# Fourteen early expert visits, one read of the last channels' matrix, and the tiles that go with them

## The chip, the cores and the metric

The kernel runs on one core of one Trainium2 chip. The metric is device microseconds (us) of one execution. In the tables, PE is TensorE's matmul stream and PEld its weight loads, DVE is VectorE, ACT is ScalarE, POOL is GpSimd and SP is SyncE; a name with a small q (SPq, POOLq) is the engine's queue, which issues DMAs and waits on semaphores. PEclk is the clock that TensorE was granted, as a share of 2.4 GHz; its two levels are 1.2 and 2.4 GHz.

## What is computed

```python
# x: 8 x 2880 x 192, fp32.  A causal 7-tap filter with softmaxed weights, one filter per head of 24 channels
out = np.einsum('hk,bskhg->bshg', w, x_unf)
x = out.reshape(23040, 192)
# 16 experts in 4 groups of 4: top-1 group, then top-1 expert in it
g_idx = np.argmax(x @ w_group, axis=1)
...
e_idx = np.argmax(xg @ w_expert[g], axis=1)
...
h = np.maximum(xg[mask_e] @ w1[g, e], 0.0)          # 192 -> 1024
ye = h @ w2[g, e]                                    # 1024 -> 192
out[tok_idx] = (g_w * e_w)[:, None] * ye
```

So each of the 23040 tokens is filtered, sent to one of 16 experts, and its expert's output is scaled by two softmax factors. The experts get between 1252 and 1628 tokens with these inputs.

## The kernel before, in words

**Routing.** The tokens are cut into 18 units of at most 12 blocks of 120 tokens. A unit (function `unit`) loads its x, filters it on TensorE with a banded matrix (L486), copies the result out with ACT (L495), transposes it, forms the logits, finds the expert on DVE, counts the position of every token in its expert's list, writes the filtered rows to a DRAM table `xcd` and scatters the token numbers into a DRAM table `idtab` by an indirect DMA of POOL (L699, with the row numbers in the small tile `rowi`, written by POOL on L678, and the token numbers in `lsi`, written by DVE on L696). A unit is a generator with 24 to 47 stages; `step()` runs one stage of one live unit.

**Visits.** The experts' work is done in visits. A visit reads one expert's matrices (`weights`): the first 128 of the 192 input channels of w1 into `ra` (512 KB), the last 64 channels into `rb`, and the two halves of w2 into `rc` (384 KB each). `rb` is filled twice from the same rows of w1, once in partitions 0 to 63 (L731) and once in 64 to 127 (L732), 256 KB each. All of these are issued on the SP queue, in order, into three `raw` buffers and three `rawc` buffers. `split` then cuts each matrix into a high part (ACT, L753, L757, L764) and the rest (DVE, L754, L758, L765), because the matmuls run in fp32r. One matmul with the high part `bh` and one with the rest `bl` take the right-hand side `xb`, whose one half of the partitions holds the high part of the last 64 channels of the tokens and whose other half holds the rest of them.

**Order.** An early visit takes tokens of an expert before all are routed. There are three portions of early visits (`VISITS`): ten experts with one slot of 256 tokens, from unit 5 on; three with two slots, from unit 9 on; three with three slots, from unit 12 on. That is 25 slots, and each is one pass of the main loop with `hidden` and `back`. While a slot runs, `advance(rate[0])` is called 16 times and runs stages of the units that are still to be routed; the rate is worked out anew at each slot:

```python
rate[0] = max(
    [(stages_to(portions[q][0]) - done[0]) / (max(starts[q] - MARGIN - i, 1) * 2 * NF)
     for q in starts if q not in idps] + [0.0])
```

with `MARGIN` 3, `NF` 8, `i` the slot that is being opened (two ahead of the one that runs) and `starts[q]` the slot at which portion q starts. A portion is opened by a read of its lists from `idtab` on the SP queue (L1197).

When all units are routed, `close_table` ends the lists: DVE writes the tile `rowi` (L948), which has the same two buffers as the units' `rowi`, and POOL scatters the end marks. Then come the wide portion (expert 0, four tiles of 128) and the last portion, in which the experts are visited in the order of what they have left (`RANKS`: the groups of tiles of each rank; `ROWS_OF`: the rows of a tile). There a group of two to four tiles goes through `hidden_pair` and `back_pair` together, eight steps a group. A branch at the end would run further visits if a rank had more tokens than its tiles hold.

Of the kernel before, what the change touches and what calls it, by code (L numbers as in the profile page):

```python
# [20 lines left out]
P = 128  # L21
BT = 120
# [15 lines left out]
def conv_moe_kernel(  # L38
# [60 lines left out]
    VISITS = ((NEED, 1, 10), (9, 2, 3), (12, 3, 3))  # L99
    portions, given = [], []  # L100
    for need, spe, n in VISITS:
        portions.append((need, tuple((len(given) + k, (2,) * spe) for k in range(n))))
        given += [2 * spe] * n
    assert len(given) == E
# [4 lines left out]
        (4, 4, 3), (4, 4, 3), (4, 4, 3), (4, 3, 3), (4, 3, 3), (4, 3, 3), (3, 3, 3), (3, 3, 3),  # L109
        (4, 4), (4, 4), (4, 3), (4, 3), (3, 3), (3, 3), (3, 2), (3, 2),  # L110
    )
    assert len(RANKS) == E
    ROWS_OF = (126, 126, 120, 120, 120, 120, 128, 124, 128, 126, 118, 114, 126, 118, 128, 116)
# [268 lines left out]
    first = [wsp.tile([P, 4, F], F32R, name="wf")]  # L382
    x_room()
    wm = const.tile([P, H], F32, name="wm")
# [48 lines left out]
    def unit(u, pre=None):  # L433
# [241 lines left out]
        rowi = rt.tile([P, 1], I32, name="rowi")  # L675
# [6 lines left out]
        def list_products():  # L682
            pl = bank("l")
            nrep = REPO if u < REPU else 1
            for k in range(nb):
                nc.tensor.matmul(
                    out=pl[:, 0:nrep * LH].rearrange("p (r n) -> p r n", r=nrep),
                    lhsT=ohl[0:Q, k // BI, :, :, k % BI].rearrange("p e l -> p (e l)"),
                    rhs=ohr[0:Q, k // BI, :, k % BI].unsqueeze(1).broadcast_to([Q, nrep, LH]),
                    start=k == 0, stop=k == nb - 1,  # L690
                )
            lv5 = rt.tile([P, LH], F32, name="lv5", bufs=1)
            lsi = rt.tile([P, LH], I32, name="lsi")
            nc.vector.tensor_scalar(
                out=lv5, in0=pl[:, 0:LH], scalar1=0.0, scalar2=float(BIG), op0=ALU.is_equal, op1=ALU.mult)
            nc.vector.scalar_tensor_tensor(  # L696
                out=lsi, in0=pl[:, 0:LH], scalar=float(t0 - 1), in1=lv5, op0=ALU.add, op1=ALU.add)

            nc.gpsimd.indirect_dma_start(  # L699
                out=TABV, out_offset=bass.IndirectOffsetOnAxis(ap=rowi.bitcast(U32), axis=0),  # L700
                in_=lsi, in_offset=None,
            )
            finished(u)
# [9 lines left out]
    def weights(r1, r2, spare=False, part=False):  # L713
# [16 lines left out]
        def load_b():  # L730
            hold(first_one, nc.sync.dma_start(out=rb[0:D2], in_=w1f[bass.ds(r1 + P, D2), :]))  # L731
            hold(first_one, nc.sync.dma_start(out=rb[D2:P], in_=w1f[bass.ds(r1 + P, D2), :]))  # L732
# [15 lines left out]
        def split(k):  # L748
            if k == 0:
                W["all"] = first.pop() if first else wsp.tile([P, 4, F], F32R, name="wf")  # L750
                W["ah"], W["al"], W["bh"], W["bl"] = (W["all"][:, q] for q in range(4))
# [3 lines left out]
            elif k == 1:  # L755
                bh, bl = W["bh"], W["bl"]
                hold(fix, pin(not fix, nc.scalar.activation(out=bh, in_=rb, func=AF.Copy)))  # L757
                hold(fix, nc.vector.tensor_tensor(out=bl, in0=rb, in1=bh.bitcast(F32), op=ALU.subtract))  # L758
# [49 lines left out]
    def turn(xs, n=2, packed=False, into=None, single=False, m=P):  # L808
# [18 lines left out]
        if packed:  # L827
            for t in range(2):
                hi, lo = slice(t * D2, (t + 1) * D2), slice((1 - t) * D2, (2 - t) * D2)
                cs = slice(t * m, (t + 1) * m)  # L830
                pb = px[hi, SLOT:SLOT + m]
                nc.scalar.activation(out=xb[hi, cs], in_=pb, func=AF.Copy)
                nc.vector.tensor_tensor(out=xb[lo, cs], in0=pb, in1=xb[hi, cs].bitcast(F32), op=ALU.subtract)  # L833
# [109 lines left out]
    def close_table():  # L943
        rows = rt.tile([P, E + 1], F32, name="rows")
        rowi = rt.tile([P, 1], I32, name="rowi")
# [482 lines left out]
    with tc.If(nrare[0] != 0):  # L1428
# [5 lines left out]
        with tc.For_i(0, nover, 1):  # L1434
            for u in range(NU):
# [5 lines left out]
                idw = rt.tile([P, LH], I32, name="lsi")[0:BT, 0:nb]  # L1441
# [72 lines left out]
```

## Time and profile before

| | |
|---|---|
| median of 3 runs | 1094.79 us (1093.23 to 1101.34) |
| the profiled execution | 1095.49 us, of which the span in the trace is 1093.7 us |
| PE busy | 1043.5 us (95%) |
| DVE, ACT, POOL busy | 676.4, 583.0, 521.4 us |
| mean granted TensorE clock | 0.986 |
| moved by DMA | 135.06 MB, 123 GB/s over the span |

Engines run beside each other, so the shares don't add up to one. TensorE's busy time is what is nearest to the span; the rows further down show in which stretches the rest of the span lies. All rows are of the one profiled execution, with times from the start of its span.

### The profile page before, as it was taken

The numbers are of one execution on the slowest core, as the hardware profiler recorded it, in microseconds if no ns is written. First come the engines' busy times: TensorE is split into PE (matmuls) and PEld (weight loads), VectorE is DVE, ScalarE is ACT, GpSimd is POOL, SyncE is SP. The second block draws the span as 40 slices with busy tenths as digits, with TensorE's granted clock in tenths as the row PEclk, the third lists the DMA queues.
The fourth block names the chain that finished last, engine by engine and source line by source line (L and its number), as shares of the span: only waits on it lengthen the run. The fifth ranks groups of instructions, "written<-read, shape, count | busy, mean of one in ns | idle before, by whom it ended". The sixth has DMA issues, their size and how long they took to land.

```text
span 1093.7 us, 20735 instructions
## 1 busy us (share of the span) xinstructions
PE 1043.5 (95%) x7116; PEld 981.0 (90%) x7116; DVE 676.4 (62%) x1646; ACT 583.0 (53%) x1346; POOL 521.4 (48%) x676
## 2 busy tenths in 40 slices
PE   6878999989999989999999999999999999999996
PEld 6756898889999889799999999999999999999996
DVE  4666887876777765666564645556466466655652
ACT  6565676676666634545454545545455455545552
POOL 3132333433333445755555554555546656657642
PEclk9998999999999989999999999999999999999998
DMA  8968799997675433432322313143233344334300
GB/s 233 252 151 222 206 244 246 234 212 181 174 181 137 105 92 110 132 100 60 93 70 79 105 40 103 45 109 94 59 105 68 85 103 111 71 85 102 92 24 24
DMA packets 122922, 135.06 MB, mean 123 GB/s; under 512 B 21147, under 2 KB 107424, under 8 KB 122810
## 3 DMA queue, kind: packets, MB, share of 16 engines
q1 hardware_dynamic: 75322, 79.89, 28.7%
q0 software_dynamic: 24160, 35.99, 12.3%
q10 hardware_dynamic: 23328, 17.80, 6.9%
q8 instruction: 57, 0.93, 0.4%
q14 instruction: 55, 0.45, 0.1%
HBM read 97.68 MB, written 36.07 MB: 122 GB/s over the span
## 4 chain that ended last, share of the span: by engine, by line
PE 79%; DMA 11%; DVE 4%; issue 2%; ACT 2%; POOL 0%; SPq 0%; POOLq 0%; ACTq 0%; DVEq 0%
PE ph L857 27%; PE po L871 10%; PE ph L887 8%; PE pm L871 8%; PE po L875 5%; PE po L905 5%; PE pm L875 3%; PE pm L486 3%; DMA xcd<-xc 3%; DMA raw<-in_moe_w 2%; PE po L909 2%; DMA out<-ys,idp 2%; DMA rawc<-in_moe_w 1%; PE ph L820 1%; DMA xg<-xcd,idp 1%
## 5 line engine op out<-in xcount | busy, mean ns | idle before, releaser
L924 POOL DMA_INDIRECT out<-ys,idp x187 | 213.1, 1140 | 271.6 <-DVE ys L934 218.6
L861 DVE SCALAR_TENSOR_TENSOR hl<-ph,hh 128x360 fp32r<-128x360 f32 (+13 forms) x328 | 189.3, 583 | 200.1 <-ACT hh L860 199.7
L860 ACT ACTIVATE hh<-ph 128x360 fp32r<-128x360 f32 (+13 forms) x328 | 167.3, 514 | 220.9 <-PE ph L857 214.4
L784 POOL DMA_INDIRECT xg<-xcd,idp x187 | 222.3, 1189 | 72.9 <-issue 28.4
L871 PE MATMUL po<-cw,hh 128*120 128x384 f32 (+6 forms) x656 | 209.7, 357 | 0.0
L857 PE MATMUL ph<-xa,wf 128*128 128x360 f32 (+13 forms) x656 | 182.6, 359 | 0.0
L857 PE MATMUL ph<-xc,wf 128*128 128x360 f32 (+13 forms) x656 | 176.1, 349 | 1.3 <-DVE xc L833 1.3
L875 PE MATMUL po<-cw,hl 128*120 128x192 f32 (+6 forms) x656 | 164.6, 251 | 0.0
L871 PE MATMUL pm<-cw,hh 128*120 128x384 f32 (+6 forms) x440 | 147.3, 356 | 0.0
L905 PE MATMUL po<-cw,hh 128*128 128x384 f32 x400 | 135.6, 389 | 0.0
L857 PEld LDWEIGHTS ph<-xc,wf 128*128 128x128 f32 x656 | 118.8, 188 | 10.6 <-DVE xc L833 1.5
L875 PEld LDWEIGHTS po<-cw,hl 128*120 128x120 f32 (+6 forms) x656 | 121.7, 186 | 3.0
L871 PEld LDWEIGHTS po<-cw,hh 128*120 128x120 f32 (+6 forms) x656 | 120.4, 184 | 2.8
L887 PE MATMUL ph<-xa,wf 128*128 128x256 f32 x600 | 118.5, 306 | 1.0 <-DVE wf L754 1.0
L857 PE MATMUL ph<-lts,wf 128*128 128x360 f32 (+13 forms) x328 | 114.9, 350 | 0.0
L875 PE MATMUL pm<-cw,hl 128*120 128x192 f32 (+6 forms) x440 | 110.3, 251 | 0.0
L909 PE MATMUL po<-cw,hl 128*128 128x192 f32 x400 | 102.0, 255 | 0.0
L857 PEld LDWEIGHTS ph<-xa,wf 128*128 128x128 f32 x656 | 100.7, 189 | 1.2
L887 PEld LDWEIGHTS ph<-xa,wf 128*128 128x128 f32 x600 | 88.5, 192 | 7.7 <-issue 2.3
L893 DVE SCALAR_TENSOR_TENSOR hl<-ph,hh 128x512 fp32r<-128x512 f32 x100 | 68.2, 685 | 41.2 <-ACT hh L892 40.9
L887 PE MATMUL ph<-xb,wf 128*128 128x256 f32 x400 | 81.9, 286 | 7.3 <-DVE xb L833 5.1
L892 ACT ACTIVATE hh<-ph 128x512 fp32r<-128x512 f32 x100 | 59.4, 598 | 53.6 <-PE ph L887 53.1
(274 smaller groups left out, 1864.2 us busy)
## 6 DMA issues: line engine op xcount, KB each, us to landing
rawc<-in_moe_w SPq DMA_DIRECT2D x66, 384.0 KB
raw<-in_moe_w SPq DMA_DIRECT2D x33, 512.0 KB
raw<-in_moe_w SPq DMA_DIRECT2D x66, 256.0 KB
xcd<-xc ACTq DMA_DIRECT2D x13, 1085.6 KB
xin<-in_x SPq DMA_DIRECT2D x7, 1134.0 KB
xin<-in_x SPq DMA_DIRECT2D x5, 1039.5 KB
xg<-xcd,idp POOLq DMA_INDIRECT x187
out<-ys,idp POOLq DMA_INDIRECT x187
```

Source lines behind the costliest of these rows:

```text
L784: nc.gpsimd.indirect_dma_start(out=xs[t][0:m, 0:XW], out_offset=None, in_=xcd[0:known, :], in_offset=bass.IndirectOffsetOnAxis(ap=ids[0:m, ...
L857: nc.tensor.matmul(out=hp, lhsT=W[wgt][:, fs], rhs=xx[:, 0:n], start=i == 0, stop=i == len(ops) - 1)
L860: nc.scalar.activation(out=hh, in_=hp, func=AF.Relu)
L861: nc.vector.scalar_tensor_tensor(out=hl, in0=hp, scalar=0.0, in1=hh.bitcast(F32), op0=ALU.max, op1=ALU.subtract,)
L871: nc.tensor.matmul(out=oo[t][0:m, 0:2 * D], lhsT=hh[:, ts], rhs=cw[:, f].rearrange("p a d -> p (a d)"), start=f == 0, stop=False,)
L875: nc.tensor.matmul(out=oo[t][0:m, 0:D], lhsT=hl[:, ts], rhs=cw[:, f, 0, :], start=False, stop=f == NF - 1,)
L887: nc.tensor.matmul(out=hp[:, j], lhsT=wgt[:, fs], rhs=xx, start=i == 0, stop=i == len(ops) - 1)
L892: nc.scalar.activation(out=hh, in_=hp, func=AF.Relu)
L893: nc.vector.scalar_tensor_tensor(out=hl, in0=hp, scalar=0.0, in1=hh.bitcast(F32), op0=ALU.max, op1=ALU.subtract,)
L905: nc.tensor.matmul(out=oo[t][:, 0:2 * D], lhsT=hh[:, j, ts], rhs=cw[:, f].rearrange("p a d -> p (a d)"), start=f == 0, stop=False,)
L909: nc.tensor.matmul(out=oo[t][:, 0:D], lhsT=hl[:, j, ts], rhs=cw[:, f, 0, :], start=False, stop=f == NF - 1,)
L924: nc.gpsimd.indirect_dma_start(out=outviews[nscat[0] % len(outviews) if view is None else view], out_offset=bass.IndirectOffsetOnAxis(ap=i ...
```

## The change

The early portions become seven experts with one slot, three with two and four with three: again 25 slots, in fourteen visits, and the last two experts get none. `RANKS` and `ROWS_OF` change with what is left for each rank; the last visit has two groups of two tiles where it had one of three and one of two. Both versions have 133 tiles in the last portion, in 40 groups, and the same sum of rows, 16300.

The last 64 channels of w1 are read once. ACT writes their high part twice, into either half of the partitions of `bh`, from the one copy; DVE forms the rest for the lower half of `bl` alone, and the upper half is zero, written once for each of the two `wf` buffers by POOL (`next_wf`). `turn` with `packed` puts both tiles' high parts into the lower half of `xb`, as the unpacked form does already. The two products that change are the rest of a weight times the rest of a token, which falls away for all tokens.

The tiles `rowi` and `lsi` of the units get four buffers instead of two, and `close_table` a tile of its own, `rowl`. The buffer of `wf` that holds the x of units 5 and 6 at first is taken ahead of the first weights' buffer instead of behind it.

```diff
-    VISITS = ((NEED, 1, 10), (9, 2, 3), (12, 3, 3))
+    VISITS = ((NEED, 1, 7), (9, 2, 3), (12, 3, 4))
...
+    given += [0] * (E - len(given))
...
-        (4, 4, 3), (4, 4, 3), (4, 4, 3), (4, 3, 3), (4, 3, 3), (4, 3, 3), (3, 3, 3), (3, 3, 3),
-        (4, 4), (4, 4), (4, 3), (4, 3), (3, 3), (3, 3), (3, 2), (3, 2),
+        (4, 4, 4), (4, 4, 3), (4, 4, 3), (4, 4, 3), (4, 4, 3), (4, 3, 3), (4, 3, 3), (3, 3, 3),
+        (4, 4), (4, 3), (4, 3), (3, 3), (3, 3), (3, 2), (3, 2), (2, 2),
...
-    ROWS_OF = (126, 126, 120, 120, 120, 120, 128, 124, 128, 126, 118, 114, 126, 118, 128, 116)
+    ROWS_OF = (124, 126, 126, 124, 120, 120, 120, 128, 118, 122, 114, 128, 124, 128, 112, 124)
...
-    first = [wsp.tile([P, 4, F], F32R, name="wf")]
     x_room()
+    wfs = [wsp.tile([P, 4, F], F32R, name="wf")]
+    nsplit = [0]
+
+    def next_wf():
+        k = nsplit[0]
+        nsplit[0] += 1
+        if k == 1:
+            wfs.append(wsp.tile([P, 4, F], F32R, name="wf"))
+        if k < 2:
+            nc.gpsimd.tensor_scalar(
+                out=wfs[k][D2:P, 3].rearrange("p (f q) -> p f q", q=P),
+                in0=ident[D2:P].unsqueeze(1).broadcast_to([D2, NF, P]), scalar1=0.0, scalar2=None, op0=ALU.mult)
+        return wfs[k % 2]
...
-        rowi = rt.tile([P, 1], I32, name="rowi")
+        rowi = rt.tile([P, 1], I32, name="rowi", bufs=4)
...
-            lsi = rt.tile([P, LH], I32, name="lsi")
+            lsi = rt.tile([P, LH], I32, name="lsi", bufs=4)
...
             hold(first_one, nc.sync.dma_start(out=rb[0:D2], in_=w1f[bass.ds(r1 + P, D2), :]))
-            hold(first_one, nc.sync.dma_start(out=rb[D2:P], in_=w1f[bass.ds(r1 + P, D2), :]))
...
-                W["all"] = first.pop() if first else wsp.tile([P, 4, F], F32R, name="wf")
-                W["ah"], W["al"], W["bh"], W["bl"] = (W["all"][:, q] for q in range(4))
+                w = next_wf()
+                W["ah"], W["al"], W["bh"], W["bl"] = (w[:, q] for q in range(4))
...
-                hold(fix, pin(not fix, nc.scalar.activation(out=bh, in_=rb, func=AF.Copy)))
-                hold(fix, nc.vector.tensor_tensor(out=bl, in0=rb, in1=bh.bitcast(F32), op=ALU.subtract))
+                for half in (slice(0, D2), slice(D2, P)):
+                    hold(fix, pin(not fix, nc.scalar.activation(out=bh[half], in_=rb[0:D2], func=AF.Copy)))
+                hold(fix, nc.vector.tensor_tensor(
+                    out=bl[0:D2], in0=rb[0:D2], in1=bh[0:D2].bitcast(F32), op=ALU.subtract))
...
-                hi, lo = slice(t * D2, (t + 1) * D2), slice((1 - t) * D2, (2 - t) * D2)
                 cs = slice(t * m, (t + 1) * m)
-                pb = px[hi, SLOT:SLOT + m]
-                nc.scalar.activation(out=xb[hi, cs], in_=pb, func=AF.Copy)
-                nc.vector.tensor_tensor(out=xb[lo, cs], in0=pb, in1=xb[hi, cs].bitcast(F32), op=ALU.subtract)
+                pb = px[t * D2:(t + 1) * D2, SLOT:SLOT + m]
+                nc.scalar.activation(out=xb[0:D2, cs], in_=pb, func=AF.Copy)
+                nc.vector.tensor_tensor(out=xb[D2:P, cs], in0=pb, in1=xb[0:D2, cs].bitcast(F32), op=ALU.subtract)
...
     def close_table():
         rows = rt.tile([P, E + 1], F32, name="rows")
-        rowi = rt.tile([P, 1], I32, name="rowi")
+        rowi = const.tile([P, 1], I32, name="rowl")
```

## Rows read from the trace of the kernel before

**Rows 1.** The page's 40 slices: TensorE's busy tenths.

```profile
PE   6878999989999989999999999999999999999996
```

**Rows 2.** Stretches: length, busy time of each engine, PEclk, DMA share, GB/s.

```profile
0.00:75.00 75.00, 57.27 (x409) 50.41 (x410) 43.55 (x205) 43.46 (x130) 17.51 (x61) 0.98 0.80 209
75.00:95.00 20.00, 14.58 (x92) 9.05 (x89) 11.01 (x44) 9.47 (x25) 10.85 (x12) 0.83 0.99 244
95.00:205.00 110.00, 103.63 (x802) 95.84 (x801) 91.13 (x211) 75.39 (x156) 35.23 (x36) 0.98 0.90 228
205.00:255.00 50.00, 46.09 (x347) 41.10 (x347) 35.81 (x84) 31.95 (x68) 18.11 (x18) 0.97 0.88 207
255.00:378.00 123.00, 123.00 (x993) 113.28 (x991) 89.19 (x230) 76.39 (x169) 48.28 (x55) 1.00 0.63 158
378.00:392.00 14.00, 8.84 (x63) 8.29 (x63) 9.75 (x36) 4.31 (x9) 6.39 (x7) 0.76 0.50 127
442.00:1059.00 617.00, 615.89 (x3868) 589.66 (x3867) 352.96 (x745) 305.52 (x710) 348.90 (x451) 1.00 0.33 85
1059.00:1094.00 35.00, 25.49 (x187) 25.20 (x185) 12.04 (x30) 10.85 (x30) 8.30 (x7) 0.91 0.08 21
```

**Rows 3.** TensorE's waits: who for whom, us in total, times, longest.

```profile
PE ph L887 <- DVE xb L833: 5.1, 1, 5.1
PE pm L820 <- DMA xg<-xcd,idp: 5.0, 1, 5.0
...
PE pm L542 <- ACT lts L535: 3.2, 2, 2.6
PE pm L486 <- DVE lsi L696: 2.7, 1, 2.7
PE ph L887 <- DVE wf L758: 2.2, 2, 1.9
```

**Rows 4.** The chain of waits around 380 us: start, length, what.

```profile
378.56 5.70 DMA idtab<-lsi,rowi
```

**Rows 5.** DVE in order of time, at the end of that wait.

```profile
384.36 0.16 DVE L948 TENSOR_TENSOR rowi<-rows,goff 128x1 int32<-128x1 f32 x1 [2.94 <-DMA idtab<-lsi,rowi]
```

**Rows 6.** The stretch behind that wait, columns as in rows 2.

```profile
384.40:391.20 6.80, 4.33 (x28) 4.24 (x29) 5.60 (x15) 0.60 (x1) 2.64 (x2) 0.50 0.34 86
```

**Rows 7.** DMA issues of the page: the 64-channel copies of w1.

```profile
raw<-in_moe_w SPq DMA_DIRECT2D x66, 256.0 KB
```

**Rows 8.** The SP queue in order of time, 166 to 172 us.

```profile
167.11 4.28 SPq L731 DMA_DIRECT2D raw<-in_moe_w  x1
171.44 0.60 SPq L732 DMA_DIRECT2D raw<-in_moe_w  x1
```

**Rows 9.** ACT in order of time, 170 to 182 us.

```profile
170.81 0.38 ACT L825 ACTIVATE xa<-pm 128x256 fp32r<-128x256 f32 x1
173.38 0.38 ACT L836 ACTIVATE xb<-pm 64x256 fp32r<-64x256 f32 x1 [2.20 <-DVE xa L826]
...
181.75 1.06 ACT L757 ACTIVATE wf<-raw 128x1024 fp32r<-128x1024 f32 x1 [2.94 <-DMA raw<-in_moe_w]
```

**Rows 10.** DVE in order of time, behind that.

```profile
182.84 1.22 DVE L758 TENSOR_TENSOR wf<-raw,wf 128x1024 fp32r<-128x1024 f32 x1 [2.74 <-ACT wf L757]
183.98 0.18 DVE L696 SCALAR_TENSOR_TENSOR lsi<-pm,lv 128x32 int32<-128x32 f32 x1
```

**Rows 11.** The chain of waits around 230 us.

```profile
224.41 14.11 DMA rawc<-in_moe_w
```

**Rows 12.** Stretches: the second slot, columns as in rows 2.

```profile
114.00:131.00 17.00, 15.14 (x112) 13.62 (x111) 16.17 (x41) 10.24 (x19) 6.56 (x6) 0.90 0.64 178
```

**Rows 13.** Groups by form: line, engine, tiles, count | busy, mean ns | idle before.

```profile
L757 ACT ACTIVATE wf<-raw 128x1024 fp32r<-128x1024 f32 x33 | 34.8, 1054 | 3.9 <-DMA raw<-in_moe_w 3.9
...
L423 POOL MEMSET xg<- 128x450 f32 x4 | 1.9, 516 | 0.0
L609 POOL CAST ohp<-ohx 120x192 f16<-120x192 bf16 x13 | 7.4, 572 | 31.9 <-DVE ohx L603 17.5 <-DVE pick L618 14.3
L678 POOL CAST rowi<-rows 128x1 int32<-128x1 f32 x18 | 4.9, 270 | 36.8 <-DMA idtab<-lsi,rowi 19.8 <-DVE rows L676 17.0
```

**Rows 14.** The SP queue's waits between 140 and 160 us.

```profile
SPq L1197 <- DMA idtab<-lsi,rowi: 8.0, 1, 8.0
```

More of the change, by code (lines that the diff above doesn't have):

```diff
@@ L1440, in conv_moe_kernel @@
                 gr = rt.tile([P, UB], F32, name="posr", bufs=1)[0:BT, 0:nb]
-                idw = rt.tile([P, LH], I32, name="lsi")[0:BT, 0:nb]
+                idw = rt.tile([P, LH], I32, name="lsi", bufs=4)[0:BT, 0:nb]
                 pn = posn[0:BT, c0:c0 + nb]
```

## The prediction, made before the changed kernel had run

> **What bounds the kernel now.** First the 40 slices [rows 1]: TensorE is busy at nine tenths or more from 270 us to the end, and below that in the first quarter. Then a table of stretches by stage [rows 2], read for idle TensorE and for a granted clock under 1. From 442 to 1059 us (the last portion) PE is busy 615.89 of 617 us at full clock, with DVE, ACT and DMA at about half or less: there only a change of PE's own work counts. From 255 to 378 us it is the same. What is not PE's own work lies elsewhere: before 75 us, 17.7 us idle; 75 to 95 us, 5.4 us idle and a clock of 0.83; 95 to 255 us (the ten one-slot visits), 6.4 + 3.9 = 10.3 us idle and a clock of 0.98 and 0.97, with DMA at 0.9; 378 to 392 us, 5.2 us idle and a clock of 0.76. Third, TensorE's waits [rows 3] name the causes: one wait of 5.1 us for xb (the one at 381 us), one of 5.0 us for the first gather, and some of 2 to 3 us on DVE and ACT results.
>
> The sum is made against the profiled execution, 1095.49 us (its span is 1093.7 us, 1.8 us lie around it); that is 0.7 us above the median of 1094.79 us. What a measurement of this kernel can tell from no change is about 1%, 11 us.
>
> **The change part by part.**
>
> *A, the tile of its own in close_table.* Unit 16's scatter into the lists is issued at 378.56 us and lands 5.70 us later [rows 4]. DVE comes to L948 before that, cannot write rowi while the scatter still reads it, and stands for 2.94 us [rows 5]; behind it in DVE's queue is the rest of an xb (L833), for which TensorE waits 5.1 us [rows 3]. Behind the wait TensorE's clock is 0.50 for 6.8 us [rows 6], which costs half of that, 3.4 us. With a tile that nobody reads the wait has no cause. Next late would be the same xb from ACT, which had long been written. A = -5.1 - 3.4 = -8.5 us; bounds -8.5 and 0 (if another small wait falls into its place).
>
> The Trainium skill, "DMA: Bandwidth & Descriptors", section "Anatomy of one DMA — SWDGE (gpsimd) path", gives about 2.0 us of fixed cost for a DMA issued by POOL. By that figure the scatter would have landed about when DVE reached L948, and A would be near nothing; the measured landing is 5.70 us, and the measurement decides.
>
> *B, less weight traffic.* 33 of the 66 copies of 256 KB fall away, and two visits whole [rows 7]. Where that matters is read from one case: L731 is issued at 167.11 us, the second copy L732 only at 171.44 us, 4.3 us later [rows 8]; ACT's L757 waits 2.94 us for it, until 181.75 us [rows 9]; DVE's L758 waits for ACT, and the small L696 stands behind it until 183.98 us [rows 10], for which TensorE waits 2.7 us [rows 3]. Without L732 the data is there some 4 us earlier, more than the wait. The second case: a w2 half takes 14.11 us to land [rows 11], ACT's split of it is late, lts is behind it, and TensorE waits 2.6 us [rows 3]; the clock of 0.97 over the 50 us around it [rows 2] is 1.5 us. In the new order the visits from slot 7 on have two slots each, so half the weights per slot there. Together 2.7 + 2.6 + 1.5 = 6.8 us; bounds -6.8 and 0, since a seven-visit stretch with weights in every slot remains. I take -5, nearer to the first, because each of the two waits hangs on a copy that goes or on a visit that now has twice the time. B = -5.
>
> *C, the start.* Up to 95 us two visits' weights are loaded, so 2 x 256 KB less; at 244 GB/s [rows 2] each is 1.1 us of DMA. The first gather, for which TensorE waits 5.0 us, shares the DMA engines with them (share 0.99). POOL's waits of 19.8 us in all before L678 [rows 13] go with the four buffers, but these lie in the start, where the chain of waits goes over xcd writes and not over POOL. Bounds -5.0 - 3.4 (the wait and its half-clock stretch, clock 0.83 over 20 us) and 0; I take -1.5, nearer to the two copies' own DMA time. C = -1.5.
>
> *D, routing pulled ahead.* The rate is a maximum over the portions not yet open. By the stage counts in unit(), 262 stages are done when slot 0 starts, unit 9 needs 345 with its overlap, and all units 753. Before, the last need rules: (753 - 265) / (20 x 16) = 1.53 stages a call, 24 a slot. After, portion 1 starts at slot 7: (345 - 265) / (2 x 16) = 2.5, 40 a slot for slots 0 and 1, then 1.4 to 1.5. So 31 stages, about 0.65 unit, move into slots 0 and 1. There DVE is the bound: 16.17 of 17 us busy in slot 1, PE idle 1.9 us and at a clock of 0.90 [rows 12]. The work is moved, not added, so PE has it later no more; what it costs is waits in order. Bounds 0 and two losses like those of slot 1 (1.9 idle + 1.7 of clock = 3.6 us each), 7.2 us. I take +2, nearer to the lower end since slots are longer by the same work. D = +2.
>
> *E, the rest of a split.* ACT has one more activation of 1024 columns over 64 partitions. Its price doesn't fall with the partitions: 64 x 256 and 128 x 256 take 0.38 us both [rows 9]. So each visit has 1.05 us more of ACT [rows 13], 31 x 1.05 = 33 us, less 7.6 us for the two visits. DVE's subtraction is taken at its old price, 1.22 us [rows 10], and can start when the first half is written, so the second lies beside it. In the last portion ACT is busy 305.52 of 617 us [rows 2] and a hidden step's results are used three steps later: 0. In the seven early visits ACT is busy 75.39 of 110 us. Bounds 0 and 7 x 1.05 = 7.4 us. I take 0.
>
> *F, zeros.* Two POOL operations of 1024 columns: between 1.2 us (a memset of 450 in 516 ns) and 3.1 us (a cast of 192 in 572 ns) each [rows 13]. The first has an idle POOL. The second waits for the x of units 5 and 6 and stands in POOL's queue among scatters and gathers; the bl product of slot 1 waits for it. Bounds 0 and 5.0 + 3.4 (as the wait of rows 3 with its clock); I take 0.
>
> *G, the last portion.* Tiles (133), groups (40) and rows (16300) are the same, so matmuls are the same in number and columns. The last group has 248 columns instead of 232, under 0.1 us a step. The stretch behind 1059 us keeps its 9.5 us without PE. 0, within 1.5 us either way.
>
> Sum: -8.5 - 5 - 1.5 + 2 = -13, 1082.5 in the profiled execution, 1081.8 beside the median. Forecast 1082.
>
> **Rivals.** (1) Only A comes: the early stretch stays bound by DVE and DMA, since seven visits in seven slots still have weights in each, and what is saved is given to D and E. 1095 - 8.5 = 1086, up to 1089. For it: DVE's 16.17 of 17 us. Against: two of the waits of rows 3 are on weights.
>
> (2) The pulled-ahead units starve TensorE once: the next unit's x or DVE's chain is late in slots 1 to 3, 5.0 us and 3.4 us as at the first gather. 1082 + 8.4 = 1090, up to 1093.
>
> (3) Slower than before: portion 1's list read (L1197) stands on the SP queue ahead of the next visit's weights. Before it stood there for 8.0 us [rows 14], in a stretch in which PE lost nothing. Now it comes two slots earlier, in one-slot visits whose DVE is already full. If the weights behind it come later than the 17 us of a slot, that visit and the following ones each lose as slot 1 did, 3.6 us over seven slots = 25 us in place of the 10.3 + 3.7 us now: +11, and with -8.5 and D's 7.2 it is 1105. It decides only from some 9 us more of wait on.
>
> (4) The wait A belongs to this execution, not to all: then its 8.5 us are not in the median. 1095 - 4.5 = 1090.
>
> (5) All goes: A, B's 6.8, C's 8.4. 1095 - 23.7 + 0 = 1071 to 1077.
>
> (6) The change doesn't do what it says, because some rank overflows its tiles and the branch runs. The tokens of the reference, counted by expert, leave 3 to 22 rows free in every rank. Left out.
>
> **How the numbers follow.** Forecast with its own range 1077 to 1086: 0.50, of which 0.40 lies below 1083.8 (1%). Rival 5: 0.15. Rival 1: 0.15. Rivals 2 and 4: 0.13. Rival 3: 0.07. Faster by over 1%: 0.40 + 0.15 = 0.55; slower by over 1%: 0.06, most of rival 3; within 1%: 0.39. The range from 1072 to 1092 leaves out rival 3, the far ends of 5 and of 2: some 2 in 10.
>
> **What would show it.** A: no wait of DVE on L948, and a clock of 1 between the last unit's end and the wide portion. B: no wait of ACT's L757 for DMA, PE idle under 6 us between the first slot and the third two-slot slot. C: the first gather lands 1 to 2 us earlier. D: units 6 to 8 scatter nearer together, then at the old pace. F: no TensorE wait for POOL's zeros in slot 1. G: PE's busy time from the wide portion to the end within 1.5 us of before. The prediction is wrong if a new wait of several us, with its half-clock stretch, appears in slots 0 to 6, or if A's place is taken by another wait on the same DVE queue.

## The result: 1% slower, where a gain of 1% was forecast

The changed kernel takes 1109.35 us (median of 4 runs, 1107.09 to 1110.00). The ratio to the kernel before, run beside it, is 1.0104, 95% interval 1.0058 to 1.0150. The forecast was 1082 us with a range up to 1092; slower had 0.06. The profiled execution took 1107.09 us, 11.6 us more than that of before. Two slow executions further down, one of e6 (2018.92 us) and one of e10 (1665.96 us), are left out of the ratios.

Where the 11.6 us went is read from a table of stretches, cut at the first matmul of each stage. This is the profile after (columns as in rows 2): the start, slots 4 to 9, slots 10 to 18, slots 19 to 21, the wide portion, the last portion.

```profile
0.00:98.10 98.10, 71.69 (x497) 59.64 (x498) 54.26 (x249) 53.58 (x155) 35.17 (x76) 0.95 0.80 203
...
165.70:249.00 83.30, 82.79 (x656) 76.18 (x655) 66.02 (x155) 63.12 (x127) 35.30 (x32) 1.00 0.84 206
249.00:377.60 128.60, 123.52 (x972) 112.58 (x970) 84.00 (x214) 76.75 (x169) 47.48 (x56) 1.00 0.53 132
377.60:409.90 32.30, 30.77 (x258) 30.32 (x255) 24.64 (x76) 15.54 (x34) 14.83 (x17) 1.00 0.41 106
...
439.20:469.80 30.60, 21.89 (x113) 19.05 (x111) 15.01 (x31) 12.56 (x25) 18.79 (x21) 0.89 0.38 92
469.80:1093.20 623.40, 622.77 (x3941) 595.49 (x3940) 353.41 (x746) 323.23 (x732) 351.90 (x439) 1.00 0.29 75
```

The same cuts in the kernel before: slots 0 to 3, then as above.

```profile
94.80:149.70 54.90, 51.25 (x396) 47.82 (x395) 46.63 (x110) 37.54 (x76) 16.69 (x17) 0.97 0.85 219
149.70:244.50 94.80, 88.18 (x683) 79.50 (x681) 74.26 (x171) 63.25 (x133) 35.52 (x35) 0.98 0.96 232
244.50:369.10 124.60, 124.60 (x983) 115.32 (x982) 87.88 (x229) 79.10 (x177) 45.78 (x53) 1.00 0.64 161
369.10:408.30 39.20, 34.04 (x272) 32.36 (x271) 26.23 (x76) 15.57 (x35) 16.79 (x19) 0.91 0.36 95
...
437.70:460.00 22.30, 19.93 (x112) 17.20 (x111) 14.34 (x31) 11.15 (x23) 16.59 (x21) 1.00 0.50 135
```

Subtract stretch by stretch. The start is +3.3 us. Slots 0 to 9 are +1.2: slots 0 to 3 longer by 12.7 (67.6 us), slots 4 to 9 shorter by 11.5, with 0.5 us of idle TensorE where there were 6.6. Slots 10 to 18 are +4.0: TensorE has less to do, 123.5 us for 124.6, but idles 5.1 us where it never did. Slots 19 to 21, with the wait of step A in them, are -6.9. The wide portion is +8.3, the last portion +1.4, the rest of the way 0.4. That makes 11.7.

TensorE's waits from slot 0 to the last portion, after (those of before are rows 3):

```profile
PE ph L836 <- DMA xg<-xcd,idp: 7.0, 2, 4.6
PE pm L557 <- ACT lts L550: 5.1, 1, 5.1
PE pm L501 <- ACT xc L510: 3.4, 4, 1.2
```

The wait for xb at the last unit's end is gone, and those on a split of weights are down to 0.7 and 0.6 us. New are 7.0 us for two gathers of the wide portion, one of 5.1 us for lts (a unit's logits on their way through ACT), and many of about 1 us for ACT's results. These three are what the experiments had to explain; a fourth loss, ahead of slot 0, comes out at e2.

**The gathers.** POOL and PE in order of time, after:

```profile
459.63 1.39 POOL L800 DMA_INDIRECT xg<-xcd,idp  x1 [0.30 <-issue]
...
461.22 0.30 PE L836 MATMUL ph<-ident,xg 124*128 124x124 f32 x1 [4.59 <-DMA xg<-xcd,idp]
```

and one step of the chain that ended last, the first after and the second before:

```profile
459.63 4.25 DMA xg<-xcd,idp
```

```profile
453.30 2.79 DMA xg<-xcd,idp
```

Behind the waits TensorE's clock is 0.50 from 461.7 to 468.5 us; its busy time in the wide portion is 21.9 us, 2.0 more than before.

These gathers are for the last portion's first rank, whose tiles now have 124 rows for 126. Grouped by the rows of their tiles (in the order of `ROWS_OF`), the 187 instructions of POOL for a gather take, as a median: 112 rows 1.02 us, 128 1.05, 126 1.08, 120 1.09, 114 1.22, 124 1.41, 118 1.72, 122 1.75. The order is not that of the sizes. The kernel before has the same figures: 1.40 for its nine gathers of 124, 1.33 for its five of 116.

**The wait for lts.** A wait of SP's queue between 100 and 145 us, after (who for whom, us, times, longest):

```profile
SPq L236 <- PE pm L501: 9.4, 1, 9.4
```

and SP, then ACT, in order of time:

```profile
128.03 0.34 SPq L236 DMA_DIRECT2D xin<-in_x  x1
128.65 0.73 SPq L746 DMA_DIRECT2D raw<-in_moe_w  x1
...
140.52 1.06 ACT L772 ACTIVATE wf<-raw 64x1024 fp32r<-64x1024 f32 x1 [5.16 <-DMA raw<-in_moe_w]
```

A unit's x load stands 9.4 us in SP's queue until the filter matmuls of an earlier unit free its buffer. A visit's rb stands behind it and lands only at 140.5 us. ACT's split waits for that, lts behind it, and TensorE for lts.

### The profile page after: what moved, and what is told of

Same layout as the page of the kernel before. It is cut to its first block, busy times and chain, and to the rows that moved or that the text cites. A ratio compares the mean times of both kernels' runs of the same rounds, so it can differ in the third digit from the quotient of the medians.

```text
span 1105.3 us, 20641 instructions
## 1 busy us (share of the span) xinstructions
PE 1044.3 (94%) x7114; PEld 977.7 (88%) x7114; DVE 669.4 (61%) x1636; ACT 610.4 (55%) x1367; POOL 541.4 (49%) x681
## 4 chain that ended last, share of the span: by engine, by line
PE 81%; DMA 8%; DVE 5%; ACT 2%; issue 2%; POOL 1%; SPq 0%; POOLq 0%; ACTq 0%; DVEq 0%
PE ph L872 27%; PE po L886 10%; PE ph L902 9%; PE pm L886 8%; PE po L920 6%; PE po L890 5%; PE pm L890 4%; PE pm L501 3%; PE po L924 2%; DMA xcd<-xc 2%; DMA out<-ys,idp 2%; PE ph L836 1%; DMA raw<-in_moe_w 1%; DMA xg<-xcd,idp 1%; PE pm L525 1%
## 5 line engine op out<-in xcount | busy, mean ns | idle before, releaser
L876 DVE SCALAR_TENSOR_TENSOR hl<-ph,hh 128x360 fp32r<-128x360 f32 (+16 forms) x328 | 189.4, 584 | 199.3 <-ACT hh L875 173.9
L875 ACT ACTIVATE hh<-ph 128x360 fp32r<-128x360 f32 (+16 forms) x328 | 166.4, 515 | 208.6 <-PE ph L872 186.6
L886 PE MATMUL po<-cw,hh 128*124 128x384 f32 (+7 forms) x656 | 210.1, 358 | 0.0
L872 PE MATMUL ph<-xa,wf 128*128 128x384 f32 (+16 forms) x656 | 183.0, 360 | 0.6 <-DVE hl L876 0.5
L872 PE MATMUL ph<-xc,wf 128*128 128x384 f32 (+16 forms) x656 | 176.6, 350 | 1.7 <-DVE xc L848 1.7
L890 PE MATMUL po<-cw,hl 128*124 128x192 f32 (+7 forms) x656 | 164.9, 251 | 0.0
L886 PE MATMUL pm<-cw,hh 128*124 128x384 f32 (+7 forms) x440 | 146.5, 357 | 0.0
L890 PEld LDWEIGHTS po<-cw,hl 128*124 128x124 f32 (+7 forms) x656 | 122.1, 186 | 3.4
L886 PEld LDWEIGHTS po<-cw,hh 128*124 128x124 f32 (+7 forms) x656 | 120.8, 184 | 3.2
L872 PE MATMUL ph<-lts,wf 128*128 128x360 f32 (+16 forms) x328 | 115.0, 351 | 0.0
L908 DVE SCALAR_TENSOR_TENSOR hl<-ph,hh 128x512 fp32r<-128x512 f32 x100 | 68.2, 685 | 39.9 <-ACT hh L907 37.1
```

The costliest lines, as they stand in the source:

```text
L872: nc.tensor.matmul(out=hp, lhsT=W[wgt][:, fs], rhs=xx[:, 0:n], start=i == 0, stop=i == len(ops) - 1)
L875: nc.scalar.activation(out=hh, in_=hp, func=AF.Relu)
L876: nc.vector.scalar_tensor_tensor(out=hl, in0=hp, scalar=0.0, in1=hh.bitcast(F32), op0=ALU.max, op1=ALU.subtract,)
L886: nc.tensor.matmul(out=oo[t][0:m, 0:2 * D], lhsT=hh[:, ts], rhs=cw[:, f].rearrange("p a d -> p (a d)"), start=f == 0, stop=False,)
L890: nc.tensor.matmul(out=oo[t][0:m, 0:D], lhsT=hl[:, ts], rhs=cw[:, f, 0, :], start=False, stop=f == NF - 1,)
L908: nc.vector.scalar_tensor_tensor(out=hl, in0=hp, scalar=0.0, in1=hh.bitcast(F32), op0=ALU.max, op1=ALU.subtract,)
```

## The experiments

All ratios are to the kernel before, run on the same chip; the lengths are of the one profiled execution, in us, cut as above.

| | ratio, 95% interval | start | slots 0-3 | 4-9 | 10-18 | 19-24 | wide | last |
|---|---|---|---|---|---|---|---|---|
| before | 1 | 94.8 | 54.9 | 94.8 | 124.6 | 68.6 | 22.3 | 622.0 |
| changed | 1.0104, 1.0058 to 1.0150 | 98.1 | 67.6 | 83.3 | 128.6 | 61.6 | 30.6 | 623.4 |
| e1 | 1.0044, 1.0017 to 1.0071 | 102.6 | 67.7 | 83.3 | 128.8 | 61.6 | 23.7 | 625.3 |
| e2 | 1.0131, 1.0080 to 1.0181 | 97.0 | 68.3 | 83.3 | 129.5 | 61.6 | 30.1 | 623.7 |
| e3 | 1.0112, 1.0065 to 1.0159 | 101.5 | 62.6 | 87.9 | 128.3 | 61.6 | 29.5 | 624.9 |
| e4 | 1.0103, 1.0068 to 1.0139 | 100.3 | 70.6 | 83.3 | 129.0 | 61.6 | 32.0 | 623.3 |
| e5 | 0.9978, 0.9951 to 1.0004 | 98.4 | 54.2 | 93.5 | 126.6 | 63.9 | 21.9 | 622.2 |
| e6 | 0.9987, 0.9959 to 1.0014 | 99.1 | 57.6 | 88.1 | 125.4 | 65.1 | 23.7 | 623.4 |
| e7 | 1.0062, 1.0040 to 1.0085 | 96.6 | 67.9 | 83.3 | 127.5 | 61.7 | 30.8 | 622.7 |
| e8 | 0.9998, 0.9976 to 1.0020 | 96.0 | 55.7 | 91.2 | 127.7 | 63.8 | 22.0 | 621.8 |
| e9 | 1.0119, 1.0069 to 1.0169 | 99.9 | 54.2 | 94.6 | 124.6 | 65.3 | 29.3 | 623.6 |
| e10 | 1.0012, 0.9977 to 1.0047 | 94.5 | 54.3 | 93.4 | 124.6 | 69.4 | 21.5 | 624.9 |
| e11 | 0.9965, 0.9940 to 0.9990 | 92.7 | 68.2 | 83.3 | 121.8 | 61.7 | 21.6 | 622.0 |
| e12 | 1.0080, 1.0048 to 1.0113 | 95.9 | 69.7 | 83.3 | 121.8 | 61.7 | 31.1 | 621.8 |
| e13 | 0.9989, 0.9969 to 1.0009 | 100.9 | 67.8 | 83.3 | 121.8 | 61.8 | 23.2 | 622.2 |
| e14 | 0.9973, 0.9949 to 0.9997 | 98.0 | 57.2 | 87.3 | 124.9 | 63.9 | 23.5 | 622.2 |

**e1, the first rank's rows.** The changed kernel with

```diff
-    ROWS_OF = (124, 126,
+    ROWS_OF = (126, 126,
```

> The changed kernel with 126 instead of 124 rows in the tiles of the first rank, and nothing else. In the changed kernel the wide group lasts from 439.2 to 469.8 us, 30.6 us against 22.3 us before, with two waits of TensorE for gathers of 124 rows (4.6 and 2.4 us) and half a clock behind them. Theory: a gather of 124 rows is slower than one of 126 (1.41 against 1.08 us on POOL), and several in a row hold up POOL. Then the waits go, the wide group lasts 22 to 24 us and the whole is 7 to 9 us shorter than the changed kernel. Rival: the first rank is late because it has twelve tiles instead of eleven, or because its list is read late; then the group stays at 29 to 31 us and the whole within 2 us.

The wide portion is 23.7 us, TensorE's waits for gathers there are 0.4 us in all, the ratio falls by 0.6%, a little less than the 7 to 9 us expected. More rows, less time.

**e9 and e10, the same in the kernel before.** The first rank gets 12 tiles, of 116 or of 120 rows:

```diff
-        (4, 4, 3), (4, 4, 3),
+        (4, 4, 4), (4, 4, 3),
-    ROWS_OF = (126, 126,
+    ROWS_OF = (116, 126,
```

> The kernel before, but its first rank has 12 tiles of 116 rows in place of 11 of 126 (6 rows more to compute, 0.2 us). Theory: the time that POOL's and the queue's work on a gather takes goes by the number of rows and how it divides, not by the bytes: gathers of 116 rows took 1.33 us of POOL in the kernel before, those of 126 1.08; the wide portion goes from 22.3 to 27 us or more, total +5 to +8 us, ratio 1.004 to 1.008. Rival: fewer rows are fewer bytes, the gather lands earlier, the wide portion stays at 21 to 23 us, ratio 0.998 to 1.002.

> The kernel before, but its first rank has 12 tiles of 120 rows in place of 11 of 126: 54 rows more to compute, at 622 us for 16300 rows 2.1 us. Theory: gathers of 120 rows took 1.09 us of POOL, as those of 126, so the wide portion stays at 22 to 24 us, though there are more rows than with 116; ratio 1.001 to 1.004, and the total is 3 to 6 us under that of the kernel with 116 rows. Rival (it is the twelfth tile, or the bytes): the wide portion is as long as with 116 rows, or longer.

TensorE's waits for gathers in the wide portion, with 116 rows and then with 120:

```profile
PE ph L820 <- DMA xg<-xcd,idp: 5.6, 2, 2.9
```

```profile
PE ph L820 <- DMA xg<-xcd,idp: 0.4, 1, 0.4
```

and the gather in the chain that ended last, in the same order:

```profile
457.02 4.34 DMA xg<-xcd,idp
```

```profile
450.92 2.77 DMA xg<-xcd,idp
```

The kernel with fewer rows is 11 us the slower, more than expected. Of these, 7.8 us lie in the wide portion; the rest is not explained (in the two profiled executions the start differs by 5.4 us, slots 19 to 24 by 4.1 the other way). Neither bytes nor the twelfth tile decide, and nothing else of the change is in these two kernels: this part is shown. All sixteen kernels of the table agree: the wide portion takes 29.3 to 32.0 us in the seven with 124 or 116 rows in the first rank, and 21.5 to 23.7 us in the nine with 126 or 120.

The Trainium skill, "DMA: Bandwidth & Descriptors", section "Why a DMA increments its semaphore by 16 and not by 1", says that a DMA is spread over the largest k up to 16 that divides the slowest dimension of its access patterns. That makes 16 for 128 and 112 rows, 15 for 120, 14 for 126, 6 for 114, 4 for 124 and 116, 2 for 118 and 122. The packets in the trace agree. A packet of a gather holds up to six rows of 772 B, so 124 rows on 4 engines would leave each with five packets of six rows and one of a single row. Summed over the 187 gathers, the rule gives the changed kernel 1649 packets of two rows, 308 of three and 268 of one; its trace has 1604, 286 and 254. POOL's times of one gather, 1.02 to 1.75 us, fall into this order too (but for 0.01 us between 120 and 126), and the landing of 4.3 us against 2.8 goes with it. Why POOL itself takes longer with fewer engines is not shown.

**e7 and e8, the two halves of the change.** e7 is the kernel before with the new `VISITS`, `RANKS` and `ROWS_OF`; e8 is the changed kernel with the old ones.

> The kernel before with the change's visits, ranks and rows alone (two reads of the last channels, no zeros, no tile of its own, two buffers). Theory: the visits bring the group of the wide portion at 124 rows (30 us instead of 22) and the pulled-ahead routing, and keep the wait of 5.1 us for xb; what they save in weight reads is 0 to 5 us; ratio 1.005 to 1.015. Rival: the visits cost nothing but those 8 us, which the fewer reads give back: ratio 0.998 to 1.002, and the loss of the changed kernel lies in the other edits.

> The changed kernel with the visits, ranks and rows of before. Theory: the tile of its own gives 8.5 us, the single read 0 to 5 us; the group of the wide portion takes 22 to 24 us as before; ratio 0.988 to 0.994. Rival: the zeros, the second activation of a split or the buffers cost what the tile gives: ratio 0.998 to 1.005, with waits of TensorE for ACT in stages 0 to 9 that the kernel before does not have.

The visits alone cost 0.6%. That they would keep the wait for xb was wrong: slots 19 to 24 take 61.7 us with the old tile. All the rest alone comes to nothing, within 0.2%, as its rival had it.

**e5, the tile alone.** The kernel before with

```diff
-        rowi = rt.tile([P, 1], I32, name="rowi")
+        rowi = const.tile([P, 1], I32, name="rowl")
```

> The kernel before, with the tile rowl of close_table alone. Theory: the wait of 5.1 us for xb and the half-clock stretch behind it lie in every execution, so stages 19 to 21 go from 39.3 to about 32 us and the total falls by 6 to 9 us, ratio 0.992 to 0.995. Rival (the fourth of the prediction): the wait belonged to the one profiled execution; ratio 0.998 to 1.002. A second rival: the scatter's end is waited for by something else next, and stages 19 to 21 stay above 36 us.

It gives 0.2%, a third of what was expected, and the interval takes in no change at all. DVE and PE at the place, in order of time:

```profile
385.21 0.15 DVE L948 TENSOR_TENSOR rowl<-rows,goff 128x1 int32<-128x1 f32 x1
...
387.71 0.50 PE L887 MATMUL ph<-xb,wf 128*128 128x256 f32 x2 [2.17 <-DVE xb L833]
```

L948 waits no more, but xb still stands in DVE's queue behind the last unit's own chain, and TensorE waits 2.2 us for it. Slots 19 to 21 take 34.6 us, between the theory's 32 and the second rival's 36. Besides, the wait is not in every execution. e10 has it (L948 stood 3.37 us). e9, with the old code there, does not: its TensorE waits 2.0 us for xb, and slots 19 to 21 take 36.0 us. So how much of the 4.6 us in e5 is the tile's own cannot be told.

**e2, e3, e4, one edit undone each.** e2 holds the zeros at their place in the program's order; e3 takes a margin of 1 for portion 1, so the pace is less uneven; e4 reads the last channels twice again and makes no zeros:

```diff
-            nc.gpsimd.tensor_scalar(
+            hold(True, nc.gpsimd.tensor_scalar(
```

```diff
-max(starts[q] - MARGIN - i, 1)
+max(starts[q] - (1 if q == 1 else MARGIN) - i, 1)
```

```diff
+            hold(first_one, nc.sync.dma_start(out=rb[D2:P], in_=w1f[bass.ds(r1 + P, D2), :]))
```

> The changed kernel with the two zeroing operations of POOL kept in the order of the program, so that the second (3.5 us) stands behind unit 4's scatter and the first gathers instead of ahead of them. Theory: it holds up that scatter, and with it the first gather and slot 0; then slot 0 starts at 94 to 96 us instead of 98.1 and the whole is about 3 us shorter. Rival: the first gather is late because the DMA engines are full (8.1 us from the scatter to the gather against 5.7 before); then slot 0 still starts at 97 to 98 us.

> The changed kernel with a margin of 1 instead of 3 slots for the first later portion, so that the routing runs at an even rate (1.5 stages a call, as before) instead of 2.5 in slots 0 and 1. Theory: the pulled-ahead load of x stands on the SP queue ahead of the weights of slot 3 until 128.0 us, the last channels' matrix lands at 140.5 us, ACT waits 5.2 us for it and TensorE 5.1 us, with half a clock behind; then this wait goes, and the whole is 5 to 9 us shorter. Rival: the single copy of 64 partitions is slow by itself or ACT is simply fuller; then a wait of 4 us or more for a weight stays in slots 1 to 4 and the whole is within 2 us.

> The changed kernel with the last channels read twice again, one activation over 128 partitions, the rest subtracted in all of them, and no zeros. Theory: the second activation (1.05 us) of every visit stands on ACT ahead of the copies that free the banks of the routing, which costs TensorE about 1 us a visit between 250 and 400 us (6.6 us of waits on xc, lg and ys, none before); then these fall below 2 us, slot 0 starts 3 us earlier because the zeros are gone, and with some 2 to 4 us more of waits on weights in slots 2 to 6 the whole is 4 to 9 us shorter. Rival: the small waits come from the shifted routing; then they stay at 5 to 7 us and the whole is 0 to 4 us shorter.

None moves the total beyond its interval. The second activation is not a loss that shows: e4 without it idles 5.2 us in slots 10 to 18, the changed kernel 5.1. The zeros' place is one, in the start. POOL in order of time, after:

```profile
69.28 3.51 POOL L394 TENSOR_SCALAR wf<-ident 64x1024 fp32r<-64x1024 f32 x1 [3.83 <-DVE lsi L711]
73.06 1.20 POOL L714 DMA_INDIRECT idtab<-lsi,rowi  x1 [0.28 <-POOL wf L394]
```

TensorE's waits for the first gathers, after and then in e2:

```profile
PE pm L836 <- DMA xg<-xcd,idp: 8.8, 2, 8.3
```

```profile
PE pm L836 <- DMA xg<-xcd,idp: 4.4, 1, 4.4
```

The second zeroing runs on POOL just ahead of the last scatter before the first gathers. That scatter starts 3.9 us after its token numbers are written, in e2 0.3 us after. It is so in every kernel: the eight in which the zeros may move have 3.9 us there and waits of 7.8 to 9.4 us for the first gathers; the eight without zeros, or with zeros held in place, have 0.3 to 0.8 us and waits of 4.4 to 5.9. In the mean that is 3.4 us of TensorE's time, less than the totals and the lengths of the start scatter by (e2 begins slot 0 at 97.0 us, not at the 94 to 96 expected). Why the gathers also follow that scatter later, after 7.0 to 8.4 us instead of 5.6 to 5.7, is open.

In e3 the rate came to 1.7 to 1.8 and not to the old 1.53, since portion 2 kept its margin of 3. The 5 us for lts went, and others of 2.5, 2.1 and 2.0 us came. From slot 0 to the wide portion e4 takes 344.6 us, the changed kernel 341.1; but e7, with two reads as well, takes 340.4, so the 3.5 us are no clear price of the second read.

**e6 and e11, the pace.** e6 is e1 with the old pace, a margin of 1 for portions 1 and 2. e11 is the kernel before with the new pace and nothing else:

```diff
-max(starts[q] - MARGIN - i, 1)
+max({1: 7, 2: 13}.get(q, starts[q]) - MARGIN - i, 1)
```

> The changed kernel with 126 rows in the first rank, and with the routing stages spread at the old rate of 1.53 a call (margin 1 for portions 1 and 2). Theory: the waits of 5 and of 1 to 3 us in the early slots come from the pace at which the routing is handed out; TensorE's idle time in stages 10 to 21 falls from 6.6 to under 3 us, from the first slot to the wide portion 330 to 336 us instead of 341, total 5 to 10 us below the kernel with 126 rows alone, ratio 0.995 to 1.000. Rival: they come from the visits themselves (fewer one-slot visits, so the same table reads and gathers in other places): 6 to 7 us of idle stay, 340 to 342 us, ratio 1.003 to 1.006.

> The kernel before, its routing stages handed out as if portion 1 began at slot 7 and portion 2 at slot 13, so at the changed kernel's rates of 2.5 and then 1.4 to 1.5 a call; the portions themselves open where they did. Theory: the pace alone costs 5 to 7 us: slots 0 to 3 take 66 us instead of 55, of which some 6 us come back as slots 4 to 9 get shorter, TensorE waits for lts once for 4 to 6 us, and small waits appear in slots 10 to 21; at the same time the wait for xb at the last unit's end goes, as that unit's scatter comes at another place (stages 19 to 21 32 to 34 us instead of 39). Ratio 1.000 to 1.006. Rival: the pace costs nothing without the new visits: from the first slot to the wide portion 335 to 338 us, ratio 0.992 to 0.997.

e6 came out as its theory had it: 0.9987 for e1's 1.0044, and 336.2 us from the first slot to the wide portion for 341.4. Slots 0 to 9 are 5.3 us shorter, slots 10 to 18 3.4, slots 19 to 24 3.5 longer.

e11's stretches (slots 0 to 3, 4 to 9, 10 to 18, 19 to 21) and its longest wait:

```profile
92.70:160.90 68.20, 59.94 (x448) 53.40 (x447) 53.30 (x137) 43.92 (x92) 19.13 (x20) 0.95 0.87 207
160.90:244.20 83.30, 82.83 (x656) 76.22 (x655) 69.12 (x158) 60.42 (x126) 37.05 (x32) 1.00 0.93 241
244.20:366.00 121.80, 121.80 (x972) 112.35 (x970) 87.57 (x219) 77.14 (x169) 47.76 (x56) 1.00 0.62 164
366.00:398.40 32.40, 30.85 (x259) 30.43 (x256) 24.89 (x76) 14.44 (x34) 14.87 (x17) 1.00 0.44 111
```

```profile
PE pm L542 <- ACT lts L535: 6.3, 1, 6.3
```

This one edit, with ten one-slot visits, two reads and the old tile, takes away the waits that steps A and B were about. In slots 4 to 9 the idle time is 0.5 us for 6.6 at a DMA share of 0.93; the stretch of the xb wait is 32.4 us for 39.2; and the total is 0.35% below before. So the pace alone suffices, and it brings its own wait for lts.

It is not the only way, though. ACT's waits for weights in slots 0 to 9, in the kernel before and then in e14 (below), which has the new visits and the single read at the old pace:

```profile
ACT cw L764 <- DMA rawc<-in_moe_w: 5.6, 2, 3.3
ACT wf L757 <- DMA raw<-in_moe_w: 3.9, 2, 2.9
```

```profile
ACT cw L780 <- DMA rawc<-in_moe_w: 2.4, 1, 2.4
ACT wf L772 <- DMA raw<-in_moe_w: 0.7, 1, 0.7
```

At the old pace these waits are 5.2 to 9.7 us in the four kernels with two reads and the old visits (before, e5, e9, e10), and 1.2 to 3.1 us in the three with the single read (e6, e8, e14). Slots 0 to 9 take 147.7 to 149.6 us in the four and 144.6 to 146.9 in the three, with 1084 to 1087 matmuls in each. So less weight traffic does, at the old pace, what B said, as far as kernels that differ in other edits too can show it.

**e12 and e13, the four buffers.** e12 is the changed kernel with two buffers of `rowi` and `lsi` again, e13 the same with 126 rows in the first rank, e14 that with the old pace.

```diff
-        rowi = rt.tile([P, 1], I32, name="rowi", bufs=4)
+        rowi = rt.tile([P, 1], I32, name="rowi")
-            lsi = rt.tile([P, LH], I32, name="lsi", bufs=4)
+            lsi = rt.tile([P, LH], I32, name="lsi")
```

> The changed kernel with two buffers of rowi and lsi in place of four. Theory: the four buffers let POOL and DVE run ahead in the start and put scatters and the zeros in another order, and this is what the changed kernel loses beyond its visits (1.0104 against 1.0062): ratio 1.004 to 1.008, first slot at 95 to 98 us. Rival: it is not the buffers: ratio 1.009 to 1.013, as the kernels with one edit undone.

> The changed kernel with 126 rows in the first rank and two buffers of rowi and lsi. Theory: the two losses are apart and add up: the wide portion 22 to 24 us in place of 30.6, no idle time of TensorE in stages 10 to 18, last portion under 623 us; total 10 to 13 us under the changed kernel, ratio 0.996 to 1.002, which leaves only the wait for lts with its half-clock stretch (6 to 10 us) between it and the forecast. Rival: the gain with two buffers was a matter of chance in the order (the visits alone, also with two buffers, had 4 us of idle time in stages 10 to 18): such idle time is back, ratio 1.003 to 1.006.

> The same with the old pace of 1.53 stages a call. Theory: the pace gives and takes: without the push the wait for lts in slots 2 and 3 goes (6 to 8 us), but the idle time of stages 4 to 9 (2.6 us in the kernel with 126 rows and the old pace, 0.6 in the changed one) and the waits after the last unit (2 to 4 us) are back; ratio 0.995 to 1.001, within 4 us of the kernel with 126 rows and two buffers. Rival: the old pace is plainly better in these visits, ratio under 0.993.

In e12 and e13 slots 10 to 18 take 121.8 us without idle time, as in e11. e13 is level with before (0.9989). With the old pace it is 0.9973, so with these visits the two paces are alike within their intervals.

Whether the buffers took the idle time away is another matter. All engines have the same instructions in the same order in e1 and e13 (by line, operation and tile); only waits differ. PE and DVE in slot 10, e1 and then e13:

```profile
261.89 0.47 PE L701 MATMUL pm<-ohr,ohl 120*128 120x32 f16 x12
...
263.30 0.19 DVE L709 TENSOR_SCALAR lv<-pm 128x32 f32<-128x32 f32 x1 [2.40 <-PE pm L701]
```

```profile
260.32 0.47 PE L701 MATMUL pm<-ohr,ohl 120*128 120x32 f16 x12
...
260.82 0.19 DVE L709 TENSOR_SCALAR lv<-pm 128x32 f32<-128x32 f32 x1 [1.50 <-PE pm L701]
```

L709 reads what the twelve L701 wrote. In e13 it starts 0.04 us after the last of them ends, in e1 0.94 us after. The update of PE's semaphore that it waits for stands in e1's trace 0.92 us after that end, in e13's 0.01 us after. In the changed kernel, e1 to e4 and e7, L709 starts 0.8 to 2.2 us late in slots 10 to 18, and all six idle 4 to 6 us there. In e11 to e13 the lag is 0.04 to 0.7 us and there is no idle time. Behind the late DVE chain an xcd write waits in ACT's queue, and the filter's copies behind it. That the late signal costs the idle time is argued from these traces, not tried by itself.

The number of buffers does not decide whether the signals are late. e5 and e9 are both the kernel before, with two buffers and the same code at this place. The same two instructions, in e5 and then in e9:

```profile
269.86 0.47 PE L686 MATMUL pm<-ohr,ohl 120*128 120x32 f16 x12
...
271.17 0.19 DVE L694 TENSOR_SCALAR lv<-pm 128x32 f32<-128x32 f32 x1 [2.34 <-PE pm L686]
```

```profile
271.03 0.47 PE L686 MATMUL pm<-ohr,ohl 120*128 120x32 f16 x12
...
271.53 0.19 DVE L694 TENSOR_SCALAR lv<-pm 128x32 f32<-128x32 f32 x1 [1.52 <-PE pm L686]
```

e5 is 0.84 us late, e9 0.04. Counted over whole traces, two groups stand apart. In the changed kernel and e1 to e8, 149 to 214 of PE's some 1300 updates of its semaphore do not stand within 0.06 us of the end of their instruction, and DVE, ACT and POOL show the same; in the kernel before and e9 to e14 it is at most one an engine. The groups go with the time of the runs and not with the code: the profile of before came first, then the result and e1 to e8, then e9 to e14. The chip is not it either, as one chip served e1 to e4, e13 and e14. The kernel before had medians of 1096.7 to 1099.0 us beside the first group and 1092.6 to 1092.7 beside the second.

So what makes the signals late is open. The idle time of slots 10 to 18 goes with them: 0.5 to 5.7 us in the first group, at most 0.4 in the second. Comparing e1 with e13, or the changed kernel with e12, changes both the buffers and the group, so it does not show what the buffers do; at the old pace, e6 with four and e14 with two are alike (0.9987, 0.9973).

## Why the prediction was wrong

**G failed first.** "Tiles (133), groups (40) and rows (16300) are the same, so matmuls are the same in number and columns. 0, within 1.5 us". In the last portion that held to 1.4 us. But the rows of a tile also set the price of its gather, and the first rank's gathers have no cover, as they come right behind the wide portion. Cost: 8.3 us, put at 0; 6.9 of them go when the first rank gets 126 rows (e1). The number stood in the trace of before, in POOL's gathers of 124 rows. G's own sign failed too: PE's busy time from the wide portion on grew by 2.7 us, most of it in the wide portion with its half clock.

**No step spoke of slots 10 to 18.** They were taken as bound by TensorE's own work, as rows 2 show from 255 to 378 us. They lost 5.1 us to idle time, 4.0 net. The idle time goes with the late signals, and that the change brought those is not shown.

**F was mis-sized.** Its mechanism was named (the second zeroing "stands in POOL's queue among scatters and gathers") and put at 0. TensorE's wait for the first gathers grew from 5.0 to 8.8 us, and the start by 3.3. The zeros took 3.51 us, above F's 3.1.

**C did not show.** It was put at -1.5, with the first gather 1 to 2 us earlier. What two reads less and four buffers give there cannot be told beside F: without zeros, or with zeros in place, kernels with either number of reads wait 4.4 to 5.9 us.

**D was mis-sized in its place, and its mechanism came.** Rival 2 foresaw one wait of 5.0 us with a stretch at half clock; the trace has 5.1 us for lts and 3.4 us at a clock of 0.50, which cost about half of that: some 6.8 us in all, near D's bound of 7.2. Behind it stood a part of rival 3, a read on SP ahead of the next weights, only that it was the x load and not L1197. Some of it comes back: TensorE's busy time in slots 0 to 9 grows by 2.4 us (3.3 in e11), in part work moved ahead from later slots. From slot 0 to the wide portion the new pace costs 1.2 us in e13 against e14, 5.1 in e1 against e6, and gives 7.8 in e11 against before.

**B held at the old pace and was wrongly added to D.** e14 has 3.1 to 5.1 us less in slots 0 to 9 than before, e9 and e10, where -5 was forecast. But the new pace alone also takes the waits of B away (e11), so the two gains are not a sum, and the new wait for lts is itself one for weights. By B's own signs it failed in the changed kernel: ACT's split of rb waits 5.2 us for a DMA, and PE idles 9.0 us in slots 0 to 9 (10.3 before) where under 6 was the sign. There the single read shows in that one wait: 5.1 to 6.4 us with one read (changed, e1, e2, e12, e13), 7.2 to 8.0 with two (e4, e7, e11). B + D was put at -3 and came to +1.2.

**A came, for another reason, and in part by luck.** Slots 19 to 21 gave 6.9 of the 8.5 us. The tile alone has 4.6 us less there (e5), since "the same xb from ACT, which had long been written" was not next late: DVE's own queue was. With the new pace the wait goes without the tile (e7, e11). Rival 4 holds in part: the wait is not in every execution, and e9 is 3.3 us shorter there without any edit.

**E held.** e4, with one activation, has the same small waits. The one sign against it is e8, whose TensorE waits 3.4 us for ACT's copies of rb (L772) in slots 0 to 9.

The best kernels here are e11 and e14, 0.35% and 0.27% under before. The lts wait behind the x load was left in e11 and the zeros ahead of the scatter in e14; neither kernel was tried without its wait. e13, with the rows put right and no late signals, still falls 12 us short of the forecast, and both of these waits are in it (8.8 and 5.3 us).

## What to carry to other kernels

When a change alters the rows of a tile, cost its gathers too, by the rows and not by the bytes, and above all those that no compute covers: 126, 120 or 128 rows, not 124 or 116. Before a wait is put down to the resource that it names, run the change's pace or order alone: one line of scheduling took away waits that had been blamed on weight traffic and on a shared tile. Then run the rest without it: less weight traffic took the first of them away as well, so the two must not be added. Look at a wait itself where totals are too coarse: 3.4 us at the first gathers are plain in sixteen traces and lost in the totals. And compare traces of runs made together: idle time that seemed to go with an edit went with the time of measuring.

## What was not expected of the hardware

One gather of 122 rows holds POOL for 1.75 us and one of 128 for 1.05; of 124 rows it lands in 4.25 us, of 126 in 2.79. Updates of semaphores came late on all compute engines in whole series of runs, whatever the kernel: in e1 DVE started up to 1.9 us after its operand was written, in e13, with the same order of instructions, 0.04 to 0.7 us after.
